# Two of Strassen's seven products, then two groups of the second layer, on TensorE

## The chip, the cores and the metric

The kernel runs on one core of one Trainium2 chip. The metric is the device time of one execution in microseconds (us). Before the change it is 2272.22 us, the median of three runs (2270.54 to 2274.28).

## What is computed

Attention over channels, then a feed-forward network with a GELU, all in fp32:

```python
qn = q / (np.linalg.norm(q, axis=1, keepdims=True) + 1e-06)      # q, k, v: 4 x 6080 x 256
kn = k / (np.linalg.norm(k, axis=1, keepdims=True) + 1e-06)
s = kn.transpose(0, 2, 1) @ qn / tau                              # 256 x 256 for each batch
a = softmax(s)
x = (v @ a).reshape(24320, 256)
h = x @ w_in                                                      # w_in: 256 x 2048
g = 0.5 * h * (1 + erf(h / sqrt(2)))
out = g @ w_out                                                   # w_out: 2048 x 256
```

## The kernel before, in words

The softmax matrix of a batch is multiplied into `w_in` once (`w_group`), so that the first layer reads v itself. That first layer, a product of 2 by 2 blocks, is done with Strassen's seven products instead of eight. Every fp32 operand is held as a rounded high part and a low rest, so one product is three matmuls (lines 416 to 418: high by high, high weight by low, low weight by high), each with its own weight load, over 512 columns of v.

The main loop at the end of `channel_attention_gelu_ffn` takes 192 **steps**: 4 batches (b) by 6 column pairs (p) by 8 pairs of rows of the hidden layer (u). The last pair of a batch has 480 columns in each half, the others 512. One step issues:

- seven **products** of the first layer, called 0 to 6 here, in the order of the list `ORDER`, by the generator `first_products`. It yields after products 0 to 5. Three PSUM banks of the pool `ps_h` (tiles `ph`) are used: `one` takes products 0, 2, 4 and 6, `two` takes 1 and 5, `three` takes 3. In between, ScalarE copies what a bank holds into SBUF (line 436: `p1` after product 0, `p5` after 1, `u2` after 2), and VectorE adds bank and copy into `h` after products 3, 4 and 5 (line 441). ScalarE then takes the GELU of `h`, or of the bank itself after product 6, twice (`gh` rounded, line 424; `g`, line 425), and VectorE forms `gl = g - gh` (line 426).
- eight **groups** of the second layer, called 0 to 7 here, by the generator `second_products`, which yields after each. A group is three matmuls (lines 486 to 488) from the blocks `gh`, `gl` of the step before into a PSUM tile `po`. Groups 0 and 1 use the block of product 3, 2 and 3 that of product 6, 4 and 5 that of product 5, 6 and 7 that of product 4.

Product 2 adds to bank `one` and so waits until `p1` is copied out of it; product 4 waits for `u2`, product 6 for the `h` made from product 4. In the last step of a pair (u = 7) the operands of the next pair are split into high and low parts between the products (`v_split`, lines 403 and 404: seven casts on ScalarE, seven subtractions on VectorE). In the first step of a pair the finished output leaves PSUM (lines 492 and 494), and sums of the next pair's v (`v_sums`, lines 387 to 393) are made on VectorE somewhat later. Between some steps come 16 more matmuls for the next batch's q and k product (`burst`, lines 177 and 179), or 12 for its weights (`w_group`, lines 352 to 354).

A scheduler takes the program in this order and may move instructions of an engine past each other where their inputs are late, so the order on each engine is shown below as built. Matmuls from before the main loop apart, TensorE's order in the main loop is nearly that of the code.

Of the kernel before, what the change touches and what calls it, by code (L numbers as in the profile page):

```python
# [51 lines left out]
def channel_attention_gelu_ffn(ctx, tc, qk, kqt, vt, tau, w_in, w_out, out):  # L52
# [342 lines left out]
    def v_split(b, p, i):  # L395
        n = PAIRS[p][1]
        x = v_blocks(b, p)
        src = {B11: x[0, 0], B21: x[1, 0], B22: x[1, 1]}.get(i)
        if src is None:
            src = vts[b, p][i - T1][:, :n]  # L400
        hi = pv.tile([P, NT], F32R, name=f"vh{i}")
        lo = pv.tile([P, NT], F32R, name=f"vl{i}")
        nc.scalar.copy(out=hi[:, :n], in_=src)
        nc.vector.tensor_tensor(out=lo[:, :n], in0=src, in1=f32(hi[:, :n]), op=ALU.subtract)
        vops[b, p, i] = hi, lo
# [23 lines left out]
    def first_products(b, p, u):  # L429

        n = PAIRS[p][1]
        out = state["blocks"] = {}

        def kept(ps, name):
            t = pg.tile([P, NT], F32, name=name, bufs=2 if name == "p1" else 1)
            nc.scalar.copy(out=t[:, :n], in_=ps[:, :n])  # L436
            return t

        def added(ps, t):
            h = pg.tile([P, NT], F32, name="h", bufs=2)  # L440
            nc.vector.tensor_tensor(out=h[:, :n], in0=ps[:, :n], in1=t[:, :n], op=ALU.add)  # L441
            return h[:, :n]

        def do(i, ps, start, stop):
            product(b, p, u, *ORDER[i], ps, start, stop)

        one = bank()
        do(0, one, True, False)
        p1 = kept(one, "p1")
        yield  # L450
        two = bank()
        do(1, two, True, False)
        p5 = kept(two, "p5")
        yield
        do(2, one, False, False)
        u2 = kept(one, "u2")
        yield
        three = bank()
        do(3, three, True, True)
        out[1, 0] = gelu(added(three, p1), n)  # L460
        yield
        do(4, one, False, False)
        out[0, 1] = gelu(added(one, p5), n)
        yield
        do(5, two, False, True)
        out[1, 1] = gelu(added(two, u2), n)
        yield
        do(6, one, False, True)
        out[0, 0] = gelu(one[:, :n], n)
# [3 lines left out]
    def second_products(b, p, u, blocks):  # L473

        t0, n = PAIRS[p]
        wo = wos.pop((b, p, u))
        for j in range(2):
            for i in (1, 0):
                gh, gl = blocks[i, j]
                for c in range(NCT):  # L480
                    if u == 0 and i == 1:
                        po[j, c] = ps_o.tile([P, NT], F32, name="po")
                    o = po[j, c][:, :n]
                    cs = slice(c * P, (c + 1) * P)
                    first, last = u == 0 and i == 1, u == NU - 1 and i == 0
                    nc.tensor.matmul(o, wo[:, 0, i, cs], gh[:, :n], start=first, stop=False)  # L486
                    nc.tensor.matmul(o, wo[:, 0, i, cs], gl[:, :n], start=False, stop=False)  # L487
                    nc.tensor.matmul(o, wo[:, 1, i, cs], gh[:, :n], start=False, stop=last)  # L488
                    if last:
                        if c == 0:  # L490
                            osb = pv.tile([P, NCT, NT], F32, name="osb", bufs=2)
                            nc.scalar.copy(out=osb[:, 0, :n], in_=o)
                        else:
                            nc.vector.tensor_copy(out=osb[:, 1, :n], in_=o)
                            t = b * N + t0 + j * n
                            dst = out[:, t:t + n].rearrange("(t p) n -> p t n", p=P)
                            step = 1 if (b, p) == (B - 1, NP - 1) else NCT
                            for h in range(0, NCT, step):
                                nc.sync.dma_start(out=dst[:, h:h + step], in_=osb[:, h:h + step, :n])
                    yield  # L500
# [5 lines left out]
    def load_unit():  # L506
        kind, g, d = units.pop(0)
        src = w_in64[:, d, g * NT:(g + 1) * NT] if kind == "in" else w_out64[:, g * 2 * C:(g + 1) * 2 * C]
        loaded.append((kind, g, d, load_w(src)))

    def narrow_unit(eng):
        kind, g, d, raw = loaded.popleft()
        if kind == "in":
            if d == 0:
                new_win(0, g)
            win = wins[0, g]
            narrow(win[:, 0, d], win[:, 1, d], raw, eng)
            if d == NCT - 1:
                nc.sync.dma_start(out=keep_in[g], in_=f32(win))
        else:  # L520
            new_wo((0, 0, g))
            wo = wos[0, 0, g]
            narrow(wo[:, 0].rearrange("p f c -> p (f c)"), wo[:, 1].rearrange("p f c -> p (f c)"), raw, eng)
            nc.sync.dma_start(out=keep_out[g], in_=f32(wo))
# [38 lines left out]
    def extras(b, p, u):  # L563

        w = p * NU + u
        nxt = (b, p, u + 3)
        if nxt[2] >= NU:
            nxt = (b, p + 1, nxt[2] - NU)
        if nxt[1] == NP:
            nxt = (b + 1, 0, nxt[2])  # L570
        if nxt[0] < B and nxt[:2] != (0, 0):
            load_wo(nxt)
        if (b, p) == (0, 0):
            if u % 2 == 1 and u // 2 + 1 < NWG:
                w_group(0, u // 2 + 1)
        if b > 0 and w == 1:
            w_group(b, NWG - 1)
        pair = (b, p + 1) if p + 1 < NP else (b + 1, 0)
        if pair[0] < B:
            if u == 1:  # L580
                load_v(*pair)
            if u in (4, 5):
                v_sums(*pair, u - 4)
        if b + 1 == B:
            return
        start, num, den = (8, 5, 2) if b == 0 else (2, 3, 1)
        for k in range(NQS // NB):
            at = start + k * num // den
            if w == at:
                for m in range(NCT):  # L590
                    burst(b + 1, k, m)
                for t in range(NB):
                    hls.pop((b + 1, k * NB + t))
            before = start + (k - 1) * num // den
            if w == (before + 1 if k else at - 1):
                for t in range(NB):
                    split_qk(b + 1, k * NB + t)
            if w == (before if k else at - 2):
                for t in range(NB):
                    load_qk(b + 1, k * NB + t)  # L600
        n0 = 8
        if n0 <= w < n0 + 2 * NCT * NSC:
            norm_part(b + 1, w - n0)
        if w == 37:
            state["stages"] = softmax(False, ps_h, "ph")
        if w >= 37:
            next(state["stages"], None)
        if w in (40, 42, 44, 46):
            load_win(b + 1, (w - 40) // 2)
        if w in (42, 44, 46):  # L610
            w_group(b + 1, (w - 42) // 2)

    steps = [(b, p, u) for b in range(B) for p in range(NP) for u in range(NU)]
    second = iter(())
    for b, p, u in steps:
        pair = (b, p + 1) if p + 1 < NP else (b + 1, 0)
        for i, _ in enumerate(first_products(b, p, u)):
            next(second, None)
            if u == NU - 1 and pair[0] < B:
                v_split(*pair, ORDER[i][1])  # L620
        if u == NU - 1 and pair[0] < B:
            v_split(*pair, ORDER[6][1])
        for _ in second:
            pass
        if (b, p) == (0, 0):
            for _ in range(2 if u < 6 else 1):
                if units:
                    load_unit()
                if loaded:
                    narrow_unit(nc.vector if len(units) % VEC == 0 else nc.gpsimd)  # L630
        extras(b, p, u)
        second = second_products(b, p, u, state.pop("blocks"))
# [30 lines left out]
```

## Time and profile before

| | |
|---|---|
| median of three runs | 2272.22 us |
| profiled execution, its own time | 2270.88 us |
| its span, first to last instruction | 2269.1 us |
| TensorE (PE) busy | 2205.5 us, 97% of the span |
| VectorE (DVE) busy | 1425.4 us, 63% |
| ScalarE (ACT) busy | 1444.4 us, 64% |
| GpSimd (POOL) busy | 82.8 us, 4% |
| chain that ended last | PE 85%, ACT 4%, DMA 4%, DVE 4% |

Matmuls are pipelined: one lasts some 0.39 us in the record, but the next starts some 0.23 us after it. The time that a matmul costs a busy TensorE is therefore read from start to start, and "idle" only says that no matmul was in flight. The step in which something stands is found by the starts of line 416, of which there are seven in a step.

### The profile page before, as it was taken

To read this page: it belongs to the slowest core of one execution; us is meant where nothing else is said; L and a number is where in the kernel's file an instruction comes from. 1 tells how busy PE (TensorE), PEld (TensorE's weight loads), DVE (VectorE), ACT (ScalarE), POOL (GpSimd) and SP (SyncE) were. 2 spreads that over 40 slices of the span, in tenths; PEclk is the share of its full clock that TensorE was granted. 3 is DMA by queue.
4 is the path that set the end of the run, shared out by engine and by line. 5 is a ranking of instruction groups with operands and counts; after the bars stand their busy time and mean duration, and the time that the engine had idled before them with its cause. 6 is when DMAs were issued, how large, how long until landed. Compare 5 with 4: busy or idle time off the path is not lost.

```text
span 2269.1 us, 26295 instructions
## 1 busy us (share of the span) xinstructions
PE 2205.5 (97%) x9648; PEld 1799.1 (79%) x9648; DVE 1425.4 (63%) x2191; ACT 1444.4 (64%) x2616; POOL 82.8 (4%) x57
## 2 busy tenths in 40 slices
PE   6778999999999999999999999999999999999999
PEld 4556787888888888888888888888888888888887
DVE  6678675765667757657567666566566655555454
ACT  4567888765766656556666566566576666666565
POOL 5242000000000000000000000000000000000000
PEclk8789999999999999999999999999999999999999
DMA  7556777532224323323133333232222221221221
GB/s 255 180 185 214 247 265 235 174 101 84 84 102 138 121 66 121 109 78 120 48 115 129 107 103 115 89 103 81 77 83 84 83 93 47 92 85 48 91 68 53
DMA packets 76481, 265.03 MB, mean 117 GB/s; under 512 B 7616, under 2 KB 9664, under 8 KB 74304
## 3 DMA queue, kind: packets, MB, share of 16 engines
q1 hardware_dynamic: 76352, 263.35, 34.5%
q8 instruction: 76, 1.25, 0.2%
q14 instruction: 53, 0.43, 0.1%
HBM read 230.03 MB, written 33.29 MB: 116 GB/s over the span
## 4 chain that ended last, share of the span: by engine, by line
PE 85%; ACT 4%; DMA 4%; DVE 4%; POOL 1%; issue 1%; SPq 0%; ACTq 0%; POOLq 0%; DVEq 0%
PE po L488 14%; PE po L486 14%; PE po L487 14%; PE ph L416 12%; PE ph L417 12%; PE ph L418 12%; DMA kqc<-kqt 3%; PE ph L177 2%; ACT kqc L199 1%; PE ph L179 1%; DMA raw<-qk 1%; ACT g L425 1%; ACT gh L424 1%; PE ph L352 1%; PE ph L353 1%
## 5 line engine op out<-in xcount | busy, mean ns | idle before, releaser
L426 DVE TENSOR_TENSOR gl<-g,gh 128x512 fp32r<-128x512 f32 (+1 forms) x768 | 522.6, 683 | 151.7 <-ACT g L425 149.7
L488 PE MATMUL po<-gh,wo 128*128 128x512 f32 (+1 forms) x1536 | 606.0, 395 | 0.0
L487 PE MATMUL po<-gl,wo 128*128 128x512 f32 (+1 forms) x1536 | 599.9, 391 | 4.1 <-DVE gl L426 4.1
L486 PE MATMUL po<-gh,wo 128*128 128x512 f32 (+1 forms) x1536 | 601.2, 392 | 0.3 <-ACT gh L424 0.3
L441 DVE TENSOR_TENSOR h<-ph,p 128x512 f32<-128x512 f32 (+1 forms) x384 | 262.5, 684 | 534.0 <-PE ph L418 423.1
L424 ACT ACTIVATE gh<-h 128x512 fp32r<-128x512 f32 (+1 forms) x576 | 361.1, 627 | 296.7 <-DVE h L441 293.5
L416 PE MATMUL ph<-vh,wh 128*128 128x512 f32 (+1 forms) x1344 | 528.3, 393 | 18.9 <-DVE wh L363 13.9
L417 PE MATMUL ph<-vl,wh 128*128 128x512 f32 (+1 forms) x1344 | 528.4, 393 | 0.0
L418 PE MATMUL ph<-vh,wl 128*128 128x512 f32 (+1 forms) x1344 | 526.1, 393 | 2.0 <-DVE wl L364 2.0
L436 ACT COPY p<-ph 128x512 f32<-128x512 f32 (+1 forms) x384 | 222.8, 583 | 271.5 <-PE ph L418 271.1
L425 ACT ACTIVATE g<-h 128x512 f32<-128x512 f32 (+1 forms) x576 | 352.1, 611 | 0.0
L487 PEld LDWEIGHTS po<-gl,wo 128*128 128x128 f32 x1536 | 288.6, 188 | 68.3 <-DVE gl L426 6.1
L488 PEld LDWEIGHTS po<-gh,wo 128*128 128x128 f32 x1536 | 288.3, 188 | 65.7
L486 PEld LDWEIGHTS po<-gh,wo 128*128 128x128 f32 x1536 | 288.4, 188 | 63.8 <-ACT gh L424 1.2
L416 PEld LDWEIGHTS ph<-vh,wh 128*128 128x128 f32 x1344 | 253.9, 189 | 85.3 <-DVE wh L363 15.1
L417 PEld LDWEIGHTS ph<-vl,wh 128*128 128x128 f32 x1344 | 253.8, 189 | 57.0
L418 PEld LDWEIGHTS ph<-vh,wl 128*128 128x128 f32 x1344 | 254.1, 189 | 55.5 <-DVE wl L364 3.4
L436 ACT COPY u<-ph 128x512 f32<-128x512 f32 (+1 forms) x192 | 111.8, 582 | 121.3 <-PE ph L418 121.3
L441 DVE TENSOR_TENSOR h<-ph,u 128x512 f32<-128x512 f32 (+1 forms) x192 | 131.1, 683 | 3.5
L425 ACT ACTIVATE g<-ph 128x512 f32<-128x512 f32 (+1 forms) x192 | 112.0, 583 | 4.6 <-DVE gl L426 4.6
L424 ACT ACTIVATE gh<-ph 128x512 fp32r<-128x512 f32 (+1 forms) x192 | 110.4, 575 | 0.0
L177 PE MATMUL ph<-hl 128*128 128x512 f32 x288 | 101.8, 395 | 0.0
(107 smaller groups left out, 1424.0 us busy)
## 6 DMA issues: line engine op xcount, KB each, us to landing
wo<-keep_out SPq DMA_DIRECT2D x184, 512.0 KB, 3.3
raw<-qk SPq DMA_DIRECT2D x95, 512.0 KB, 4.2
kqc<-kqt SPq DMA_DIRECT2D x60, 512.0 KB, 4.5
v_raw<-vt SPq DMA_DIRECT2D x20, 1024.0 KB, 5.3
out<-osb SPq DMA_DIRECT2D x40, 512.0 KB, 3.3
win<-keep_in SPq DMA_DIRECT2D x12, 1024.0 KB, 4.8
kqc<-kqt SPq DMA_DIRECT2D x12, 480.0 KB, 4.5
raw<-w_in SPq DMA_DIRECT2D x8, 512.0 KB, 4.6
```

Source lines behind the costliest of these rows:

```text
L177: nc.tensor.matmul(s, hl[:, 0, j, 0, cs], hl[:, :, j, 1], start=(i == 0), stop=False, skip_group_check=True)
L416: nc.tensor.matmul(ps[:, :n], wh, hi[:, :n], start=start, stop=False, skip_group_check=True)
L417: nc.tensor.matmul(ps[:, :n], wh, lo[:, :n], start=False, stop=False, skip_group_check=True)
L418: nc.tensor.matmul(ps[:, :n], wl, hi[:, :n], start=False, stop=stop, skip_group_check=True)
L424: nc.scalar.activation(out=gh[:, :n], in_=src, func=AF.Gelu)
L425: nc.scalar.activation(out=g[:, :n], in_=src, func=AF.Gelu)
L426: nc.vector.tensor_tensor(out=gl[:, :n], in0=g[:, :n], in1=f32(gh[:, :n]), op=ALU.subtract)
L436: nc.scalar.copy(out=t[:, :n], in_=ps[:, :n])
L441: nc.vector.tensor_tensor(out=h[:, :n], in0=ps[:, :n], in1=t[:, :n], op=ALU.add)
L486: nc.tensor.matmul(o, wo[:, 0, i, cs], gh[:, :n], start=first, stop=False)
L487: nc.tensor.matmul(o, wo[:, 0, i, cs], gl[:, :n], start=False, stop=False)
L488: nc.tensor.matmul(o, wo[:, 1, i, cs], gh[:, :n], start=False, stop=last)
```

## The change

In the main loop the second layer's generator was advanced once after each of products 0 to 5. Now it is advanced not at all after products 0, 2 and 4 and twice after products 1, 3 and 5. Groups 6 and 7 still follow product 6.

```diff
         for i, _ in enumerate(first_products(b, p, u)):
-            next(second, None)
+
+            for _ in range(i % 2 * 2):
+                next(second, None)
             if u == NU - 1 and pair[0] < B:
                 v_split(*pair, ORDER[i][1])
```

So with D for a product and G for a group a step was D0 G0 D1 G1 D2 G2 D3 G3 D4 G4 D5 G5 D6 G6 G7 and is now D0 D1 G0 G1 D2 D3 G2 G3 D4 D5 G4 G5 D6 G6 G7.

**TensorE, a step in the middle** (batch 2, pair 0, u = 4), its first twelve matmuls. `vh0`, `vl0` are the operands of product 0, `vh3`, `vl3` those of product 1; `wh2`, `wl2` are weights of the first layer, `wo` of the second. Before:

```order
L416 MATMUL ph_11191<-vh0_10662,wh2_102 128x512
L417 MATMUL ph_11191<-vl0_10663,wh2_102 128x512
L418 MATMUL ph_11191<-vh0_10662,wl2_106 128x512
L486 MATMUL po_10871<-gh_11131,wo_10859 128x512
L487 MATMUL po_10871<-gl_11133,wo_10859 128x512
L488 MATMUL po_10871<-gh_11131,wo_10859 128x512
L416 MATMUL ph_11200<-vh3_10675,wh2_102 128x512
L417 MATMUL ph_11200<-vl3_10676,wh2_102 128x512
L418 MATMUL ph_11200<-vh3_10675,wl2_106 128x512
L486 MATMUL po_10881<-gh_11131,wo_10859 128x512
L487 MATMUL po_10881<-gl_11133,wo_10859 128x512
L488 MATMUL po_10881<-gh_11131,wo_10859 128x512
```

With the change:

```order
L416 MATMUL ph_11191<-vh0_10659,wh2_102 128x512
L417 MATMUL ph_11191<-vl0_10660,wh2_102 128x512
L418 MATMUL ph_11191<-vh0_10659,wl2_106 128x512
L416 MATMUL ph_11197<-vh3_10675,wh2_102 128x512
L417 MATMUL ph_11197<-vl3_10676,wh2_102 128x512
L418 MATMUL ph_11197<-vh3_10675,wl2_106 128x512
L486 MATMUL po_10877<-gh_11128,wo_10859 128x512
L487 MATMUL po_10877<-gl_11130,wo_10859 128x512
L488 MATMUL po_10877<-gh_11128,wo_10859 128x512
L486 MATMUL po_10881<-gh_11128,wo_10859 128x512
L487 MATMUL po_10881<-gl_11130,wo_10859 128x512
L488 MATMUL po_10881<-gh_11128,wo_10859 128x512
```

Product 1 comes one block of three matmuls earlier, group 0 one block later; all others of the step stand where they stood (the same holds for product 3 with group 2 and product 5 with group 4).

**VectorE, the same step**, the additions `h` after products 3, 4 and 5 and the three subtractions `gl` that belong to them (the first `h` reads `p1`, the second `p5`, the third `u2`; the first `gl` belongs to the first `h`). Before:

```order
L441 TENSOR_TENSOR h_11221<-ph_11217,p1_11195 128x512
L441 TENSOR_TENSOR h_11235<-ph_11191,p5_11204 128x512
L426 TENSOR_TENSOR gl_11225<-g_11224,gh_11223 128x512
L441 TENSOR_TENSOR h_11249<-ph_11200,u2_11212 128x512
L426 TENSOR_TENSOR gl_11239<-g_11238,gh_11237 128x512
L426 TENSOR_TENSOR gl_11253<-g_11252,gh_11251 128x512
```

With the change:

```order
L441 TENSOR_TENSOR h_11218<-ph_11214,p1_11195 128x512
L426 TENSOR_TENSOR gl_11222<-g_11221,gh_11220 128x512
L441 TENSOR_TENSOR h_11235<-ph_11191,p5_11201 128x512
L441 TENSOR_TENSOR h_11246<-ph_11197,u2_11212 128x512
L426 TENSOR_TENSOR gl_11239<-g_11238,gh_11237 128x512
L426 TENSOR_TENSOR gl_11250<-g_11249,gh_11248 128x512
```

The first `gl`, which waits for both GELUs of the block from product 3, now stands ahead of the `h` after product 4, for which product 6 waits.

**VectorE, the first step of a pair** (batch 2, pair 1, u = 0), from the `h` after product 3 to the `h` after product 5. Before:

```order
L441 TENSOR_TENSOR h_11633<-ph_11629,p1_11605 128x512
L387 TENSOR_TENSOR vs0_12112<-v_raw_11813 128x512
L494 COPY osb_11627<-po_10881 128x512
L426 TENSOR_TENSOR gl_11637<-g_11636,gh_11635 128x512
L441 TENSOR_TENSOR h_11649<-ph_11601,p5_11614 128x512
L441 TENSOR_TENSOR h_11663<-ph_11610,u2_11622 128x512
```

With the change:

```order
L441 TENSOR_TENSOR h_11628<-ph_11624,p1_11605 128x512
L387 TENSOR_TENSOR vs0_12112<-v_raw_11813 128x512
L388 TENSOR_TENSOR vs2_12114<-v_raw_11813 128x512
L494 COPY osb_11639<-po_10881 128x512
L426 TENSOR_TENSOR gl_11632<-g_11631,gh_11630 128x512
L441 TENSOR_TENSOR h_11649<-ph_11601,p5_11611 128x512
L441 TENSOR_TENSOR h_11660<-ph_11607,u2_11622 128x512
```

One more sum of v (line 388) has moved ahead of the `h` after product 4; `osb` and the first `gl` stood ahead of it already.

## Rows read from the trace of the kernel before

**Rows 1.** The page, part 1 and one line of part 2.

```profile
PE 2205.5 (97%) x9648; PEld 1799.1 (79%) x9648; DVE 1425.4 (63%) x2191; ACT 1444.4 (64%) x2616; POOL 82.8 (4%) x57
...
PEclk8789999999999999999999999999999999999999
```

**Rows 2.** Stretches: us, then busy (xcount) of PE, PEld, DVE, ACT, POOL; PEclk, DMA share, GB/s.

```profile
230.00:430.00 200.00, 197.39 (x871) 158.49 (x870) 131.09 (x209) 171.55 (x322) 0.00 (x0) 1.00 0.75 246
430.00:2190.00 1760.00, 1760.00 (x7791) 1443.86 (x7791) 1089.48 (x1676) 1092.35 (x1979) 0.00 (x0) 1.00 0.28 93
```

**Rows 3.** PE timeline: start us, us, engine, line; first instruction of three steps.

```profile
1257.56 0.40 PE L416 MATMUL ph<-vh,wh 128*128 128x512 f32 x1
...
1267.93 0.39 PE L416 MATMUL ph<-vh,wh 128*128 128x512 f32 x1
...
1278.35 0.39 PE L416 MATMUL ph<-vh,wh 128*128 128x512 f32 x1
```

**Rows 4.** PE timeline of the step after those; the last row opens a burst.

```profile
1283.93 0.39 PE L416 MATMUL ph<-vh,wh 128*128 128x512 f32 x1
...
1286.69 0.39 PE L416 MATMUL ph<-vh,wh 128*128 128x512 f32 x1
...
1287.38 0.39 PE L486 MATMUL po<-gh,wo 128*128 128x512 f32 x1
...
1288.77 0.40 PE L177 MATMUL ph<-hl 128*128 128x512 f32 x1
```

**Rows 5.** PE timeline near the start: six groups in a row, then two products in a row.

```profile
164.43 0.40 PE L486 MATMUL po<-gh,wo 128*128 128x512 f32 x1
...
168.63 0.39 PE L486 MATMUL po<-gh,wo 128*128 128x512 f32 x1
...
192.34 0.40 PE L416 MATMUL ph<-vh,wh 128*128 128x512 f32 x1
...
193.73 0.39 PE L488 MATMUL po<-gh,wo 128*128 128x512 f32 x1
```

**Rows 6.** PE timeline, 480 columns: three steps apart, then eight groups apart.

```profile
2220.59 0.38 PE L416 MATMUL ph<-vh,wh 128*128 128x480 f32 x1
...
2250.01 0.38 PE L416 MATMUL ph<-vh,wh 128*128 128x480 f32 x1
...
2258.50 0.38 PE L486 MATMUL po<-gh,wo 128*128 128x480 f32 x1
...
2263.78 0.38 PE L486 MATMUL po<-gh,wo 128*128 128x480 f32 x1
```

**Rows 7.** Timeline, batch 2, pair 1, first step: DVE, ACT, and PE at product 6.

```profile
1317.48 0.69 DVE L441 TENSOR_TENSOR h<-ph,p 128x512 f32<-128x512 f32 x1 [2.85 <-ACT osb L492]
...
1318.74 0.62 ACT L425 ACTIVATE g<-h 128x512 f32<-128x512 f32 x1
...
1319.39 0.69 DVE L426 TENSOR_TENSOR gl<-g,gh 128x512 fp32r<-128x512 f32 x1
...
1320.00 0.68 DVE L441 TENSOR_TENSOR h<-ph,p 128x512 f32<-128x512 f32 x1
...
1320.44 0.40 PE L488 MATMUL po<-gh,wo 128*128 128x512 f32 x1
1320.73 0.50 PE L416 MATMUL ph<-vh,wh 128*128 128x512 f32 x1
...
1321.07 0.39 PE L417 MATMUL ph<-vl,wh 128*128 128x512 f32 x1
```

**Rows 8.** Timeline, a plain step (batch 2, pair 0, u = 4): DVE, ACT, PE.

```profile
1273.07 0.69 DVE L441 TENSOR_TENSOR h<-ph,p 128x512 f32<-128x512 f32 x1 [4.14 <-PE ph L418]
...
1274.33 0.61 ACT L425 ACTIVATE g<-h 128x512 f32<-128x512 f32 x1
...
1274.45 0.69 DVE L441 TENSOR_TENSOR h<-ph,p 128x512 f32<-128x512 f32 x1 [0.69 <-ACT gh L424]
...
1276.27 0.39 PE L416 MATMUL ph<-vh,wh 128*128 128x512 f32 x1
```

## The prediction

> **What bounds the kernel now.** I read the page first: TensorE is busy in 97% of the span and runs at the full one of its two clock levels, 2.4 GHz, behind the first slices [rows 1]. The table of stretches says where the other 3% lie: between 430 and 2190 us TensorE has 1760.00 of 1760.00 us in flight, between 230 and 430 us it lacks 2.61 of 200 [rows 2]. The rest is the start, where weights are made, and the tail, where there is nothing left to overlap. So in the main loop no engine can give TensorE work faster than it takes it, and only two things can change the time: how far apart its matmuls start, and waits that are too short to show as idle time.
>
> The timeline of TensorE gives the first. A step has 45 matmuls. A step that follows a burst takes 1267.93 - 1257.56 = 10.37 us, the next one, with another step ahead of it, 1278.35 - 1267.93 = 10.42 [rows 3]. Same work, no idle time, and yet 0.05 us apart: **the spacing depends on what was issued before.** The step behind these shows how. Its first eight blocks of three take 1283.93 - 1278.35 us for 24 matmuls, 0.2325 us each; the next four take 1286.69 - 1283.93 for 12, 0.2300 each; its last two groups, which stand in a row, take 1288.77 - 1287.38 for six, 0.2317 each [rows 3, 4]. Products and groups in turn thus settle at 0.2300, and two groups in a row at the step's end spoil that for some eight blocks. Near the start six groups in a row take 168.63 - 164.43 for 18 matmuls, 0.2333 each, and two products in a row take 193.73 - 192.34 for six, 0.2317 each [rows 5]. With 480 columns three steps take 2250.01 - 2220.59 for 135 matmuls, 0.2179 each, and eight groups in a row 2263.78 - 2258.50 for 24, 0.2200 each [rows 6]. In both widths the quickest spacing is that of strict turns, the slowest that of one kind alone.
>
> **The change, part by part.** No instruction is added or removed. In each step products 1, 3 and 5 move one block earlier and groups 0, 2 and 4 one block later.
>
> *Waits of TensorE.* Products 0, 2, 4 and 6 keep their distances of four blocks, so the copies `p1`, `u2` and the `h` for product 6 have the time they had. Groups 0, 2 and 4 come later and so wait less. Products 1 and 3 need their banks one block earlier; both banks were read by VectorE in the step before, several microseconds ago, and after a burst its 16 matmuls lie between. I cost these at nothing.
>
> *Order on VectorE.* The first `gl` now stands ahead of the `h` that product 6 waits for. In a plain step [rows 8] the first `h` would start 0.69 us earlier, at 1272.38, since product 3 comes one block earlier and VectorE sat idle. The second GELU then ends at 1274.33 + 0.61 - 0.69 = 1274.25, `gl` starts some 0.05 us later, `h` another 0.61 later (1320.00 - 1319.39, [rows 7]) at 1274.91 and ends at 1275.60. Product 6 starts at 1276.27, so 0.67 us are left: no cost while nothing else is queued on VectorE.
>
> In the first step of a pair something is. There `h` started at 1320.00, ended at 1320.68, and product 6 started at 1320.73, 0.29 us after the matmul ahead of it, its own second matmul 0.34 later: 0.63 where 0.46 is usual, a wait of 0.17 us [rows 7]. I found this wait in five of the pairs' first steps. With the change the first `h` starts at 1317.48 - 0.69 = 1316.79. Behind it stand two sums, `osb`, `gl` and the `h` in question, each some 0.60 us after the one before: `gl` at 1319.20, by when its GELU (1318.74 + 0.62 - 0.69 = 1318.67) is done, and `h` from 1319.80 to 1320.49. Product 6 is due 0.23 after 1320.44, at 1320.67, so the wait goes, by a margin of 0.18 us, of which the signal takes 0.05 (1320.68 to 1320.73). Gain: 5 x 0.17 = 0.8 us. If the margin fails in all 23 such steps, the loss is 23 x 0.17 = 3.9 us; the margin speaks for the gain.
>
> Trainium skill, PSUM — Partial Sum Buffer, Engine vs sequencer instructions: the queues of ScalarE and VectorE are strictly first in, first out. By that a `gl` that is not ready holds up the `h` behind it, which speaks against this change; the margins above already carry it.
>
> *ScalarE at the start of batch 0.* Between 230 and 430 us the 2.61 us idle come from squares of q and k that wait for a transfer and hold the copies `p1` and `u2` queued behind them. The change moves `p5` next to `p1`, and some squares past the copies, in both directions. Bounds: a gain of 2.6, a loss of as much; I take nothing.
>
> *Spacing on TensorE.* The new order, pairs of products and pairs of groups, nowhere runs long enough in this trace. Bounds are the rows for strict turns, 0.2300, and for one kind alone, 0.2333. I take 0.2317, since both rows of two blocks of one kind in a row show it. A step is then 45 x 0.2317 = 10.43 us. Now a step takes 10.42 where another step stands ahead of it and 10.37 after a burst; the bursts come every third step in three of four batches, which makes 10.405 on average. Per step +0.022, for some 150 of the 160 steps of 512 columns, those behind the start, **+3.3 us**. For the 32 steps of 480 columns I take halfway between 0.2179 and 0.2200, as the rows there show only turns and one kind alone: 32 x 45 x 0.00105 = **+1.5 us**.
>
> Sum: 3.3 + 1.5 - 0.8 = **+4.0 us** on the profiled execution's 2270.9, or 2274.9. The median of the runs lies 1.3 above that execution, so the forecast for the median is 2276.2 us, say 2276.
>
> Trainium skill, TensorE: Matmul & The Clock Gate, Back-to-back issue gap: at 2.4 GHz a matmul's distance to the next is its columns over 2.4 plus 2.5 ns, 215.7 ns for 512 columns, with nothing in it for what stands next to it. By that rule the term for the spacing would be nothing and the sum -0.8. The rows speak against it: at 512 columns and the same clock they show 230.0 to 233.3.
>
> **The rivals.**
>
> *Slower: the pairs never settle.* The place is TensorE, every step. If each change between two of a kind and one of the other keeps the matmuls at 0.2325, as behind the two groups at a step's end, a step takes 10.46, which is +0.058 x 150 = 8.6, with the other terms +9.3: 2281.5 for the median. If pairs cost as much as one kind alone, 0.2333, it is +14.0, the 480-column steps +3.0, together +16.2: 2288. This decides from a spacing of 0.2318 on. For it: unsettled blocks last eight blocks after one irregularity, and the new step has one at product 6 with its lone place between two pairs of groups. Against it: the pairs are themselves regular, and both pair rows show less.
>
> *Faster: the pairs settle as turns do.* If they lock in at 0.2300, a step takes 10.35, -0.055 x 150 = -8.3, with the waits -9.1: 2263 for the median. For it: the order repeats every four blocks for twelve of fifteen. Against it: every row with two of a kind in a row is slower.
>
> *No change at all: spacing that goes by columns alone*, or that averages to what it is. Then only the waits change, -0.8 with bounds of -3.4 and +6.5 from the two terms on VectorE and ScalarE: 2271.4 for the median. That the scheduler undoes the change is excluded by its order on TensorE.
>
> **How the numbers follow.** About 0.2%, 4.5 us, is what a measurement of this kernel can tell from no change. Within it lie my forecast (pairs at 0.231 to 0.2317) and the case of no change, together 0.42; the slower rival has 0.40, since its bound is only 0.0001 us away from the value I took; the faster one 0.18. The range leaves out the outer half of the faster rival and the quarter of the slower one in which pairs cost as much as one kind alone: 2264 to 2285.
>
> **What would show it right or wrong.** In the changed profile: TensorE again without idle time from 430 to 2190 us; a middle step of 10.43 us from one first product to the next, the same after a burst and after a step; six matmuls of two groups in a row in 1.39 us; product 6 in a pair's first step 0.23 us behind the matmul ahead of it. The forecast is wrong if steps of 512 columns take under 10.39 or over 10.44 us, or if product 6 or product 3 begins to wait in plain steps. If the time between 230 and 430 us moves by more than 2.6 us, ScalarE's order there was underrated.

## The result, and the profile after

The changed kernel takes **2281.55 us** (median of 8 runs, 2278.41 to 2283.36), the kernel before in the same session 2272.82 us (8 runs, 2270.54 to 2275.68). The ratio is 1.0038, 95% interval 1.0028 to 1.0047: slower by 8.7 us. The profiled execution took 2280.79 us, with a span of 2279.0.

The page of the changed kernel, its part 1, one line of part 2 and one of part 4:

```profile
PE 2216.3 (97%) x9648; PEld 1801.8 (79%) x9648; DVE 1427.7 (63%) x2191; ACT 1429.7 (63%) x2616; POOL 82.7 (4%) x57
...
PEclk8789999999999999999999999999999999999999
...
PE 86%; DVE 4%; DMA 3%; ACT 3%; POOL 1%; issue 1%; SPq 0%; ACTq 0%; POOLq 0%; DVEq 0%
```

Same instructions, same share, same clock as in [rows 1]; TensorE is busy for 2216.3 - 2205.5 = 10.8 us longer, VectorE for 2.3 us longer, ScalarE for 14.7 us less. The table of stretches says what kind of loss that is (columns as in [rows 2]):

```profile
230.00:430.00 200.00, 196.60 (x857) 155.37 (x856) 128.69 (x203) 167.73 (x317) 0.00 (x0) 1.00 0.74 243
430.00:2190.00 1760.00, 1760.00 (x7759) 1440.19 (x7758) 1086.95 (x1671) 1074.87 (x1969) 0.00 (x0) 1.00 0.28 92
```

From 430 to 2190 us TensorE is in flight all the time, as before, at a granted clock of 1.00, but gets 7759 matmuls done instead of 7791 [rows 2]. No wait was added: from batch 1's first matmul to that of the last pair of batch 3, starts over 0.26 us apart add up to 0.5 us beyond the usual 0.23 each, and to 1.4 us in the kernel before. The matmuls stand further apart. Between 230 and 430 us 0.8 us more are idle. The same three steps as in [rows 3, 4], on TensorE's timeline:

```profile
1263.91 0.39 PE L416 MATMUL ph<-vh,wh 128*128 128x512 f32 x1
...
1274.36 0.39 PE L416 MATMUL ph<-vh,wh 128*128 128x512 f32 x1
...
1275.74 0.40 PE L486 MATMUL po<-gh,wo 128*128 128x512 f32 x1
...
1277.15 0.39 PE L416 MATMUL ph<-vh,wh 128*128 128x512 f32 x1
...
1284.82 0.39 PE L416 MATMUL ph<-vh,wh 128*128 128x512 f32 x1
```

The step behind a burst takes 1274.36 - 1263.91 = 10.45 us (before 10.37), the plain one 10.46 (before 10.42). Inside it six matmuls of two products take 1275.74 - 1274.36 = 1.38 us, six of two groups 1277.15 - 1275.74 = 1.41. The starts in ns make that 1382 and 1404: 0.2303 and **0.2340 us a matmul**, and the next pairs of the step repeat it.

Product 6 in the first step of a pair, on VectorE (DVE) and TensorE, batch 2, pair 1, as in [rows 7]:

```profile
1326.45 0.69 DVE L441 TENSOR_TENSOR h<-ph,p 128x512 f32<-128x512 f32 x1
...
1327.14 0.39 PE L488 MATMUL po<-gh,wo 128*128 128x512 f32 x1
...
1327.36 0.39 PE L416 MATMUL ph<-vh,wh 128*128 128x512 f32 x1
1327.59 0.39 PE L417 MATMUL ph<-vl,wh 128*128 128x512 f32 x1
```

`h` ends at 1327.14, 0.22 us before product 6 starts, and the starts are 0.22 and 0.23 apart: no wait. All five such waits of the kernel before are gone. In batch 0 there are still waits behind ScalarE (ACT), the longest here for product 2:

```profile
294.86 1.05 ACT L199 ACTIVATE kqc<-kqc 128x1024 f32<-128x1024 f32 x1
...
296.74 1.06 ACT L199 ACTIVATE kqc<-kqc 128x1024 f32<-128x1024 f32 x1 [0.74 <-DMA kqc<-kqt]
...
296.97 0.40 PE L488 MATMUL po<-gh,wo 128*128 128x512 f32 x1
...
297.80 0.56 ACT L436 COPY p<-ph 128x512 f32<-128x512 f32 x1
...
298.42 0.50 PE L416 MATMUL ph<-vh,wh 128*128 128x512 f32 x1 [1.05 <-ACT p L436]
```

A square waits for its transfer, the copy `p1` stands behind it, and product 2 starts 1.45 us after the matmul ahead of it.

### The profile page after: what moved, and what is told of

Read it like the earlier page. It is cut to its first block, busy times and chain, and to the rows that moved or that the text cites. A ratio compares the mean times of both kernels' runs of the same rounds, so it can differ in the third digit from the quotient of the medians.

```text
span 2279.0 us, 26202 instructions
## 1 busy us (share of the span) xinstructions
PE 2216.3 (97%) x9648; PEld 1801.8 (79%) x9648; DVE 1427.7 (63%) x2191; ACT 1429.7 (63%) x2616; POOL 82.7 (4%) x57
## 4 chain that ended last, share of the span: by engine, by line
PE 86%; DVE 4%; DMA 3%; ACT 3%; POOL 1%; issue 1%; SPq 0%; ACTq 0%; POOLq 0%; DVEq 0%
PE po L486 14%; PE po L488 14%; PE po L487 14%; PE ph L417 13%; PE ph L416 12%; PE ph L418 12%; PE ph L177 3%; DMA kqc<-kqt 3%; PE ph L179 1%; ACT kqc L199 1%; DMA raw<-qk 1%; ACT g L425 1%; ACT gh L424 1%; PE ph L352 1%; PE ph L353 1%
```

## The experiments

Theory: the time is lost in the spacing of TensorE's matmuls, by their order. First rival: it is lost in batch 0, in waits behind ScalarE. All kernels were timed beside the kernel before. For each the table has the ratio, the plain step and the step behind a burst of the timeline above, and the time from batch 1's first matmul to that of the last pair of batch 3 (136 steps), each from two starts of the first line of `product`. Starts are printed to 0.01 us, so these differences are good to 0.01.

| kernel | ratio to before, 95% | plain step | behind a burst | 136 steps |
|---|---|---|---|---|
| before | | 10.42 | 10.37 | 1500.12 |
| the change | 1.0038 (1.0028 to 1.0047) | 10.46 | 10.45 | 1506.22 |
| change in batches 1 to 3 | 1.0023 (1.0014 to 1.0032) | 10.46 | 10.45 | 1506.11 |
| change in batch 0 | 1.0008 (1.0000 to 1.0017) | 10.42 | 10.36 | 1500.06 |
| one pair, early | 1.0005 (0.9997 to 1.0014) | 10.41 | 10.43 | 1501.46 |
| one pair, late | 1.0018 (1.0010 to 1.0027) | 10.42 | 10.44 | 1502.67 |
| turns of single matmuls | 1.0139 (1.0125 to 1.0153) | 10.61 | 10.59 | 1524.85 |
| pairs, groups in one bank | 1.0038 (1.0026 to 1.0050) | 10.46 | 10.44 | 1506.28 |
| turns, tail in one bank | 1.0005 (0.9996 to 1.0013) | 10.42 | 10.36 | 1500.30 |
| turns, high-high-low | 1.0009 (1.0001 to 1.0018) | 10.42 | 10.36 | 1500.66 |
| pairs, aligned | 0.9990 (0.9981 to 0.9998) | 10.39 | 10.39 | 1497.70 |
| turns, aligned | 1.0011 (1.0002 to 1.0020) | 10.44 | 10.43 | 1503.34 |
| turns, products off | 0.9976 (0.9967 to 0.9985) | 10.35 | 10.37 | 1495.07 |
| pairs, products off | 0.9994 (0.9985 to 1.0003) | 10.37 | 10.44 | 1497.75 |

The last column repeats well: the four kernels that run the turns of the kernel before there, in whatever bank or order inside a block, have it within 0.60 us of each other. Its first and last start in the kernel before, then with the change:

```profile
680.88 0.40 PE L416 MATMUL ph<-vh,wh 128*128 128x512 f32 x1
...
2181.00 0.38 PE L416 MATMUL ph<-vh,wh 128*128 128x480 f32 x1
```

```profile
684.59 0.40 PE L416 MATMUL ph<-vh,wh 128*128 128x512 f32 x1
...
2190.81 0.37 PE L416 MATMUL ph<-vh,wh 128*128 128x480 f32 x1
```

### Where: the later batches alone, the first alone

```diff
-            for _ in range(i % 2 * 2):
+            for _ in range(i % 2 * 2 if b > 0 else 1):
```

> The change in batches 1 to 3 alone, turns in batch 0. Theory of the spacing (the two orders differ in how far apart TensorE's matmuls start, in every step of 512 columns): a plain step of batches 1 to 3 takes 10.46 us instead of 10.42, and the kernel loses what the two traces part by behind step 48, 6.2 us, a ratio of 1.0027; TensorE is in flight for 197.4 us between 230 and 430 us, as in the kernel before. Rival, the waits (the time is lost in batch 0, where copies for the products queue behind squares on ScalarE): at most 1 us is lost here, a ratio under 1.0005.

```diff
-            for _ in range(i % 2 * 2):
+            for _ in range(i % 2 * 2 if b == 0 else 1):
```

> The change in batch 0 alone, turns in batches 1 to 3. Theory of the spacing: 3.7 us are lost, what the two traces part by at step 48, a ratio of 1.0016; of it some 2 us are waits of products 2, 4 and 6 between 220 and 460 us, the rest is spacing, and from batch 1 on a plain step takes 10.42 us. Rival, the waits: nearly all of the 8.7 us is lost here, a ratio over 1.003.

The changed later batches, from batch 1's first matmul to that of the last pair:

```profile
682.17 0.40 PE L416 MATMUL ph<-vh,wh 128*128 128x512 f32 x1
...
2188.28 0.37 PE L416 MATMUL ph<-vh,wh 128*128 128x480 f32 x1
```

and with batch 0 alone changed:

```profile
684.91 0.40 PE L416 MATMUL ph<-vh,wh 128*128 128x512 f32 x1
...
2184.97 0.38 PE L416 MATMUL ph<-vh,wh 128*128 128x480 f32 x1
```

1506.11 against 1500.06 us: +6.0 us sit in the 136 steps, where no matmul waits more than before, and the later batches alone cost 5.2 us by the times of the runs. The rival falls: it needed nearly all of the loss in batch 0. Batch 0 gives 1.8 us (0 to 3.9), less than the 3.7 expected. How much of that is ScalarE's queue can't be told: from the first step to batch 1 the kernel before took 581.64 us, the one with batch 0 as before 584.91, the two with pairs there 587.24 and 587.36. The first two issue batch 0 in the same order on every engine, and differ by 3.3 us. Nor did the 197.4 us in flight expected between 230 and 430 us come: the kernel with batch 0 as before has 196.78 there, the two with pairs 196.60 and 194.63. Steps 28 to 47, behind those waits, take 225.02 us in pairs and 224.00 to 224.06 in turns; this 1.0 us is spacing.

### How much disorder it takes

```diff
-            for _ in range(i % 2 * 2):
+            for _ in range((0, 2, 1, 1, 1, 1)[i]):
```

> Only the first two products and the first two groups of a step in pairs (D0 D1 G0 G1), turns behind them. If one irregular place unsettles the eight blocks behind it, as the two groups at a step's end do in the kernel before, the quick stretch of a step shrinks from blocks 9 to 12 and little more to the last blocks ahead of the step's end: a plain step takes 10.45 us, and this one pair brings most of the loss, 4 to 6 us. If each of three pairs costs the same: 10.43 us, 2 us.

```diff
-            for _ in range(i % 2 * 2):
+            for _ in range((1, 1, 1, 1, 0, 2)[i]):
```

> Only the last full pair of a step (D4 D5 G4 G5), turns ahead of it. One pair at a step's start left a plain step at 10.41 us, since it stood where the turns had not settled yet, and cost only the steps behind a burst. Here it stands in the settled stretch. If an irregular place unsettles what follows, that stretch is lost: a plain step takes 10.45 to 10.47 us, 4 to 7 us in all. If what counts is the number of pairs, each a third of the change's 0.04 us: 10.43 us, 2 us.

Early, then late; first instruction of three steps, the first of them behind a burst:

```profile
1259.07 0.40 PE L416 MATMUL ph<-vh,wh 128*128 128x512 f32 x1
...
1269.50 0.39 PE L416 MATMUL ph<-vh,wh 128*128 128x512 f32 x1
...
1279.91 0.39 PE L416 MATMUL ph<-vh,wh 128*128 128x512 f32 x1
```

```profile
1263.40 0.39 PE L416 MATMUL ph<-vh,wh 128*128 128x512 f32 x1
...
1273.84 0.39 PE L416 MATMUL ph<-vh,wh 128*128 128x512 f32 x1
...
1284.26 0.39 PE L416 MATMUL ph<-vh,wh 128*128 128x512 f32 x1
```

Both expectations fall for the plain step: it takes 10.41 and 10.42 us, no more than in turns. The step behind a burst loses 0.06 to 0.07, and with the late pair a step that ends in a burst loses 0.04. In sum the 136 steps lose 1.3 and 2.6 us, not far from the 2 us of an equal share, and the late pair's ratio, 4.1 us (2.3 to 6.1), reaches into the 4 to 7 of the other theory; but neither has the loss where it lies. A pair costs nothing in the plain steps, where all three together cost 0.04 us: the spacing is no sum over places.

In the third of these kernels each matmul of a product is followed by one of a group:

```diff
         nc.tensor.matmul(ps[:, :n], wh, hi[:, :n], start=start, stop=False, skip_group_check=True)
+        next(second[0], None)
...
                     nc.tensor.matmul(o, wo[:, 0, i, cs], gh[:, :n], start=first, stop=False)
+                    yield
```

> Turns of single matmuls: one of a product, one of a group, and so on; the last group alone at the end. If the quick spacing comes from changing between products and groups as often as can be, matmuls start 0.2300 us apart or less, a plain step takes 10.35 us or less, and the kernel is quicker than the one before by 8 us, less new waits. If it comes from regular turns of three and three, any other order costs 0.2325 or more: 10.46 us, slower by 6 us or more. Product 2 starts with two matmuls less between it and the end of product 0 and product 6 likewise behind product 4, 0.46 us; the rival of the waits expects waits of product 6 in plain steps, and a loss of 5 us or more from these alone.

```profile
1284.90 0.39 PE L416 MATMUL ph<-vh,wh 128*128 128x512 f32 x1
...
1295.51 0.39 PE L416 MATMUL ph<-vh,wh 128*128 128x512 f32 x1
```

10.61 us, 0.236 us a matmul, the widest of all, with no wait in this step. More changes of kind are not better. The kernel loses some 32 us (1.39%); 24.7 of them sit in the 136 steps.

### What in a block sets it: bank, weights

Second theory: what costs is the change of the PSUM bank, or what helps is loading the same weights twice in a row. In the first two kernels the groups of the second layer are reordered, so that two in a row add to one tile `po` (everywhere; in turns, at the step's end alone); in the third the matmuls of each block, of products and of groups, come as high by high, low weight by high, high weight by low.

```diff
-        for j in range(2):
-            for i in (1, 0):
+        for j, i, c in [(j, i, c) for j in (0, 1) for c in (0, 1) for i in (1, 0)]:
...
```

> The change, with the eight groups in another order, so that the two groups of a pair go to the same PSUM tile (six matmuls in a row into one bank). If the spacing depends on how often matmuls change the bank they add to, the pairs of groups come from 0.2340 us a matmul down to 0.2303, what pairs of products show, and a plain step takes at most 10.41 us instead of 10.46, no slower than the kernel before. If it depends only on products and groups, their weights and operands, nothing moves: 10.46 us, ratio 1.0038. The block of product 6 is needed three matmuls earlier; waits for it would show as starts over 0.26 us apart in the first pair of groups, in steps that split operands above all.

```diff
-        for j in range(2):
-            for i in (1, 0):
+        for j, i, c in ((0, 1, 0), (0, 1, 1), (0, 0, 0), (0, 0, 1), (1, 1, 0), (1, 0, 0), (1, 1, 1), (1, 0, 1)):
...
```

> Turns as before the change; only the last four groups are reordered, so that the two groups that stand in a row at a step's end go to one PSUM tile. If the change of bank is what unsettles the turns, the tail no longer does, all blocks settle at 0.2300 and a plain step takes 10.35 us instead of 10.42: 8 us quicker, ratio 0.9965. If not, 10.42 us and a ratio of 1.000.

```diff
-        nc.tensor.matmul(ps[:, :n], wh, lo[:, :n], start=False, stop=False, skip_group_check=True)
-        nc.tensor.matmul(ps[:, :n], wl, hi[:, :n], start=False, stop=stop, skip_group_check=True)
+        nc.tensor.matmul(ps[:, :n], wl, hi[:, :n], start=False, stop=False, skip_group_check=True)
+        nc.tensor.matmul(ps[:, :n], wh, lo[:, :n], start=False, stop=stop, skip_group_check=True)
...
```

> Turns as before the change; in every block of three the second and third matmul trade places, so that the two with the same weights no longer follow each other but the two with the same moving operand do. If two loads of the same weights in a row make the quick spacing, it is lost: 0.2325 or more, a step of 10.46 us or more, 6 us slower or worse. If only the bank and the kind matter: 10.42 us, ratio 1.000 within 0.001.

A plain step of the first and of the third:

```profile
1273.47 0.39 PE L416 MATMUL ph<-vh,wh 128*128 128x512 f32 x1
...
1283.93 0.39 PE L416 MATMUL ph<-vh,wh 128*128 128x512 f32 x1
```

```profile
1267.52 0.39 PE L416 MATMUL ph<-vh,wh 128*128 128x512 f32 x1
...
1277.94 0.39 PE L416 MATMUL ph<-vh,wh 128*128 128x512 f32 x1
```

10.46 as in the change, 10.42 as before it, and 10.42 with the tail in one bank: the starts agree with the unreordered kernels to 1 or 2 ns nearly everywhere in the step. Neither the bank nor the repeated weights set the spacing. The second theory falls. (The ratio of 1.0009 for the third need not be spacing: its interval begins at 1.0001, and its trace has new waits of products 6 and 2 behind VectorE and ScalarE in the first two steps of the last pair of batch 2, some 1.5 us.)

### The operand's address

One difference between the kinds had not been varied. As built, the moving operands of products start at multiples of 64 bytes in a partition (`vh0` at 141504), those of groups 32 bytes over one (`gh` at 204512). Third theory: the order matters because the kinds read from differently placed tiles. Eight more fp32 words in a tile ahead of `gh`, `gl` move these by 32 bytes; in a tile ahead of `vh`, `vl` they move both kinds. The weights stay where they were; other tiles behind the padding (`p1`, `h`, `g`) move along. The order of instructions on every engine stays as it was.

```diff
-            state["nsum"] = pm.tile([P, 2 * NCT, NSC], F32, name="nsum")
+            nsum = pm.tile([P, 2 * NCT * NSC + 8], F32, name="nsum")
+            state["nsum"] = nsum[:, :2 * NCT * NSC].rearrange("p (t c) -> p t c", t=2 * NCT)
```

> The change, with 32 bytes of padding ahead of the tiles that the second layer reads. As built, products and groups differ in one thing that no earlier run varied: the moving operands of products start at multiples of 64 bytes in a partition (vh0 at 141504), those of groups 32 bytes over one (gh at 204512). The padding puts gh, gl at multiples of 64 too. Theory of the operand's address (groups space their matmuls wider because of it, and the order of products and groups matters only since the two kinds differ): in the step of mixed widths products take 216 ns at 480 columns, which is 229.3 at 512, where groups take 234; with the padding groups come to 0.2293 as well, a plain step takes 10.32 us or less instead of 10.46, and the kernel is at 2258 us or below, a ratio to the kernel before of 0.994 or less. If the address means nothing: 10.46 us, ratio 1.0038.

> Turns as before the change, with the same 32 bytes of padding. Theory of the operand's address: a plain step takes the same 10.32 us or less as with pairs, no step differs by what stands ahead of it, and the change no longer costs anything beside this kernel (within 0.1%); ratio to the kernel before 0.994 or less. If the address means nothing: 10.42 us, ratio 1.000.

```diff
-        raw = pv.tile([P, NCT, 2 * NT], F32, name="v_raw")
+        raw = pv.tile([P, NCT * 2 * NT + 8], F32, name="v_raw")[:, :NCT * 2 * NT].rearrange("p (t n) -> p t n", t=NCT)
```

> Turns as before the change, with the padding placed earlier, so that the operands of products start 32 bytes over a multiple of 64 (vh0 at 141536) and those of groups at multiples of 64: the two kinds trade places. Theory of the operand's address: products become the wide kind and groups the narrow one, 0.233 to 0.235 against 0.229 or less in the same-kind stretches; a plain step stays near 10.4 us, between the aligned kernel and all operands off. If the address means nothing: spacing matmul by matmul as in the kernel before, 10.42 us, ratio 1.000.

> The change, with the padding that puts the operands of products 32 bytes over a multiple of 64 and those of groups at multiples of 64. So far each placing of the operands has its own spacing for each order: as built, turns 10.42 and pairs 10.46 us a plain step; both kinds at multiples of 64, turns 10.43 and pairs 10.39; products off, turns 10.35. If what counts is that two blocks of the kind that is off stand in a row (as built, two groups in a row take 0.2340 us a matmul in the steady pairs, two products 0.2303), the two trade places here: products in a row 0.2340, groups in a row 0.2303, a plain step 10.43 to 10.46 us, 12 to 16 us slower than turns with the same padding and 2 to 8 us slower than the kernel before. If the kind that is off means nothing and it is the padding as such that brought the gain: 10.35 us, as turns with the same padding.

Batch 1's first matmul and that of the last pair, for pairs aligned, turns aligned (line 416 is 417 here), turns and pairs with products off:

```profile
680.97 0.39 PE L417 MATMUL ph<-vh,wh 128*128 128x512 f32 x1
...
2178.67 0.37 PE L417 MATMUL ph<-vh,wh 128*128 128x480 f32 x1
```

```profile
681.83 0.39 PE L417 MATMUL ph<-vh,wh 128*128 128x512 f32 x1
...
2185.18 0.37 PE L417 MATMUL ph<-vh,wh 128*128 128x480 f32 x1
```

```profile
679.78 0.40 PE L416 MATMUL ph<-vh,wh 128*128 128x512 f32 x1
...
2174.85 0.38 PE L416 MATMUL ph<-vh,wh 128*128 128x480 f32 x1
```

```profile
683.10 0.39 PE L416 MATMUL ph<-vh,wh 128*128 128x512 f32 x1
...
2180.85 0.38 PE L416 MATMUL ph<-vh,wh 128*128 128x480 f32 x1
```

Where the tiles lie decides, though not as the theory had it. With both kinds at multiples of 64, pairs need 1497.70 us where turns need 1503.34: **the change is now 5.6 us quicker** than its own turns, where as built it is 6.1 slower. Their medians are 2270.13 and 2274.85 us. With products off, pairs cost 2.7. The sizes expected fell: 10.39 and 10.44 us a plain step instead of 10.32; 10.35 instead of near 10.4 for turns with products off; and 10.37 instead of 10.43 to 10.46 for pairs with products off, which lose mostly behind bursts (10.44 against 10.37).

What did hold is which kind is wide. Mean distance from a matmul's start to the next, in ns, over three steps that do not follow a burst (63 matmuls of products, 72 of groups):

| | products | groups |
|---|---|---|
| as built (groups off): turns, pairs | 230.1, 230.8 | 232.8, 233.8 |
| both aligned: turns, pairs | 232.4, 230.2 | 231.4, 231.6 |
| products off: turns, pairs | 231.7, 232.5 | 228.4, 228.6 |

The kind that lies 32 bytes off is the wide one both times. It isn't the whole account: with both aligned either kind can be the wider, and in turns the products, whose tiles had not moved, went from 230.1 to 232.4 ns when those of the groups did.

Is it the operands, or the other tiles that moved along? The last ten groups of the program stand in a row behind all products. As built the first eight of them take 0.2200 us a matmul [rows 6]; the same starts in the aligned pairs:

```profile
2256.05 0.38 PE L487 MATMUL po<-gh,wo 128*128 128x480 f32 x1
...
2261.29 0.38 PE L487 MATMUL po<-gh,wo 128*128 128x480 f32 x1
```

That is 5.24 us for 24 matmuls, 0.2183 each, and the last 24 distances of the program are 0.2183 to 0.2184 in all four kernels with padding, 0.2200 in the kernel before and in the change. In two stretches of 1 us and more VectorE and ScalarE stand idle there, and the distances don't change. So the operand's address moves the spacing without a change of kind and without work on those engines. It isn't alone in that: in the turns of single matmuls, without padding, the last 16 matmuls of such a row come 0.2179 us apart (3268 ns for 15 distances), behind one start that was 0.27 us after the one ahead of it. One address thus has more than one settled spacing.

Turns with products off are quicker than both kernels: 2266.69 us, ratio 0.9976 (0.9967 to 0.9985) to the kernel before.

## Why the prediction was right, and where it was wrong

The time lies within the range, but not with the forecast: 2276.0 was 5.5 us too low, and a step of 10.46 us is over the 10.44 at which the prediction called its forecast wrong. The range holds because it took in most of the slower rival. What came has that rival's price: a plain step of 10.46 us and 2281.5 us, measured 10.46 and 2281.55. That the times agree this closely is luck: the rival's +9.3 us meets a measured +8.7, on a kernel before that was 0.6 us slower beside it than in the runs that the forecast started from. Nor is it the rival's mechanism, pairs that never settle at 0.2325: the pairs do settle, the same from step to step to 1 or 2 ns, with products at 0.2303 and groups at 0.2340.

- **Frame**: right. TensorE is still in flight from 430 to 2190 us without a gap, so spacing and short waits were the things to cost.
- **Product 6**: right. The waits of the five first steps of pairs are gone, 0.8 us, and the margin of 0.22 us is close to the 0.18 worked out.
- **Spacing of 512 columns**: the step that failed. It took 0.2317 us "since both rows of two blocks of one kind in a row show it". Those rows were single pairs that came behind other things: the two groups of [rows 4] stand behind settled turns, and in a steady run of pairs two groups take 0.2340; two products, 0.2317 in [rows 5], take 0.2303. The step takes 0.2324 us a matmul, not 0.2317. Of the traces' 6.1 us in the 136 steps, 0.8 was gained by the waits and 16 steps of 480 columns cost 16 x 0.02 = 0.3; so 120 steps of 512 columns lost 6.6 us, 0.055 each. Over the prediction's 150 steps this term is +8.2 instead of +3.3.
- **480 columns**: sign right, size too large. A step takes 9.83 us instead of 9.81, for 32 steps 0.6 us and not 1.5.
- **ScalarE in batch 0**: left at 0 with 2.6 either way. The idle time there grew by 0.8 us. The runs bound it but don't settle it, since the same order of batch 0 differs by 3.3 us between two executions.

With the corrected terms the sum is 8.2 + 0.6 - 0.8 = 8.0 us, against 8.7 measured (interval 6.4 to 10.7).

The rival in which spacing goes by columns alone is refuted: one width at one granted clock shows steps from 10.35 to 10.61 us. The Trainium skill, TensorE: Matmul & The Clock Gate, Back-to-back issue gap, gives the rule quoted in the prediction for an isolated matmul, and for a stream in which each matmul has its weight load some 131 ns at 512 columns. The runs, with 230.0 to 235.8 ns a matmul in these steps, differ from both. The reasoning "products and groups in turn settle" was a fact of this placing of tiles and not of turns: aligned, turns are the wider order.

## What to carry to other kernels

Where TensorE never waits, a new order still has a price, here of some tenths of a per cent and 1.4% at the most: read it from start to start, over whole periods in their steady state, and not from a few matmuls that stand behind another pattern. Before an order of matmuls is judged, look at the byte at which its operands start; a pad of 32 bytes moved this kernel as much as the order did, and turned the sign of the change. Cost a step by classes (plain, behind a burst), since each has its own spacing.

## What the runs showed of the hardware

The distance between matmuls of 512 columns (fp32r, each with its own weight load) is not fixed: in these steps most lie between 224 and 243 ns and repeat from step to step to 1 or 2 ns. It changes with the order of products and groups (10.42 to 10.61 us a plain step) and with a shift of the moving operand by 32 bytes (10.46 to 10.39 in pairs), and not with the bank that is added to or the order of the three matmuls in a block (10.46 and 10.42 as without).

Trainium skill, SBUF — State Buffer, Specifications (TRN2): SBUF has lines of 16 bytes, and each crossing to a new one costs. By that alone a shift of 32 bytes would change nothing, as both places are multiples of 16; the runs, 10.46 against 10.39 us for a plain step in pairs, show a change that it does not explain.

Why the address and the order act together is open. Other shifts, and moving the weights alone, were not tried; no run here shows what in TensorE or SBUF makes the distance.
